# Attention and two mixture-of-experts layers: separate key and query sources, later gates, two token tiles by a product

## The chip, the cores and the metric

The kernel runs on one core of one Trainium2 chip. The time is that of one execution on the device in microseconds; the profiled execution has records of TensorE (PE, with its weight loads PEld), VectorE (DVE), ScalarE (ACT), GpSimd (POOL), and of the issues on SyncE's queue (SPq) and GpSimd's (POOLq).

## The reference

Three stages follow each other. Inputs are float32: q, k, v of 4 batches x 8 heads x 576 positions x 64, and s of 4 x 8 x 576.

```python
scores = q @ k.T / sqrt(64)
cum    = cumsum(max(s, 0))
bias   = -(cum[:, None] - cum[None, :])
scores = where(causal, -1e9, scores + min(bias, 0))
x      = softmax(scores) @ v              # as 2304 tokens x 512
h      = x @ w_in                         # 512 x 2048
x2     = (h * clip(h + 3, 0, 6) / 6) @ w_out   # 2048 x 512
logits = x2 @ w_gate                      # 8 experts
# the (token, expert) logits in falling order; a token goes to the first
# expert with room; each expert has room for 288 tokens
out[token] = max(x2[token] @ w1[e], 0) @ w2[e]  # 512 x 1024 x 512
```

## The kernel before

All products run in 16-bit parts: a float32 value is split into a high part (scaled by 64) and a low part, and three products (high x high, high x low, low x high) are summed in PSUM.

**Order.** The kernel is Python that emits instructions; a list scheduler of the tile framework then fixes the order on each engine when the program is built. Priority is the order of emission; an instruction whose inputs or buffer slots are expected later lets others go ahead. A block under `tc.high_priority` is put before what was emitted up to 20000 places earlier, `tc.issue_after(x)` (in `behind`) keeps an instruction behind `x` on its own engine. On the chip each queue then runs in its fixed order. So that stages overlap, `merge` (line 62) takes turns between generators, each of which yields the cost of what it has emitted: the one whose share of its total or budget is smallest goes next, a negative yield makes a stream rest for so many ns of the others' work, and a yielded condition blocks it until it holds.

**Attention.** A pair of heads of one batch is a unit n (16 pairs, 9 blocks of 128 rows). In step t (line 751, 18 steps), `row_stage` works on pair t, `col_stage` on t - 1, `pv_stage` on t - 2, and `prep(t + 1)` (line 234) is emitted ahead of them. `prep` builds from the loaded q and k one source tile `kq` (one buffer) with three parts of 9 x 128 columns: the low product's keys with constants, the keys with their cumulative sums CT, and the queries; a second tile `qb` (two buffers) takes the queries for the low product. One DMA transpose (line 253, 27 blocks of 128 x 128) makes `kqT` of `kq`. `row_stage` (line 286) makes the scores by rows, takes maxima on VectorE, writes them into `qb`, and a transpose of 9 blocks makes `qB` (line 334). `col_stage` (line 342) makes the scores by columns, with the maxima subtracted by the product itself, and the exponentials; `pv_stage` (line 392) the outputs, and a transpose of 10 blocks (line 442) makes `xT`, the input of the MLP. Loads of the next pairs are emitted by `between` (line 723) at the end of `row_stage`. All loads and transposes are issued on SP's queue.

**MLP and weights.** `prologue` (line 670) loads the 16 raw blocks of w_in and w_out (1 MB each) and decodes them to 16-bit parts (`decode`, line 495; the low part on GpSimd in line 517), with a budget for each step (PB, line 18). `mlp` (line 634) takes units u of 256 tokens: eight `h_step`s (line 548: 24 products of 256 columns, line 556) and two `x2_tile`s (line 591: 48 products of 512 columns, lines 598 to 600; the output goes to `xo`, two slots, from there to DRAM as `x2d` and, for the first ten tiles, through a transpose to the gate). Its budget in a step is FILL = 15500. An x2 tile waits for each half of w_out as it is decoded. What is left of the MLP after the attention runs alone.

**Gates.** For the last eight tiles the logits are taken from the MLP's hidden values by w_out x w_gate, so that routing can begin before x2 is there. `gates` (line 685) makes that product for 16 blocks of w_out: `gate_product` (line 522) issues two DMA transposes of 4 blocks (line 527) into `wT` (one slot), rests 2500 ns, and emits 8 small matmuls (lines 531, 532). GB = 1200 is its budget in a step, GT0 = 2 the first step in which it has one; a block also waits until its part of w_out is decoded.

**Experts.** `route` and `tail` (lines 952 and 1032) pick the 288 tokens of each expert, under high priority, beside the last eight x2 tiles. `gather(0)` fetches the first expert's tokens from `x2d` (three indirect DMAs on GpSimd), `tokens(0)` transposes them to `xt` (line 1119), behind the weight loads emitted before it. To start before the last tile is stored, `x2d` holds zeros for tile 17 (line 853); its tokens, always the last of the list, are put in by a product with a 0/1 matrix `lastsel` (128 x 128, lines 1052 to 1057 and 1208 to 1213), then the tile is stored for the other experts. Line 1128 is the experts' matmul, line 1106 the low part of their weights on GpSimd; `load` and `convert` (lines 1081, 1096) bring the weights through three staging slots, and the load of the second expert's third block, the last ahead of the xt transposes, waits for the fourth block of the first expert to be converted.

## Time and profile before

| | |
|---|---|
| three timed runs | 930.39, 931.59, 936.60 us; median 931.59 |
| profiled execution | 931.17 us, of which the span from first to last instruction 929.4 us |
| busy | PE 834.4 us (90%), DVE 568.3 (61%), POOL 472.6 (51%), ACT 374.9 (40%) |
| mean granted TensorE clock | 0.949 |

The profile is one execution. Busy times of an engine are the union of its instructions; matmuls are pipelined, so a busy PE need not be at its peak. In rows of a group the number behind the bar is idle time just before the instruction and what ended it. Where a row reads `[11.41 <-DMA kqT<-kq]`, the engine stood idle for 11.41 us until that DMA had landed. A granted clock of 1.00 is 2.4 GHz, 0.50 is 1.2 GHz, and a value between is a mean over a stretch.

### The profile page before, as it was taken

Reading aid. Unit: us, or ns where it says so; the run is one execution under the profiler, and the core shown is the slowest. Engines: PE = TensorE matmul, PEld = TensorE weight load, DVE = VectorE, ACT = ScalarE, POOL = GpSimd, SP = SyncE. Lnnn points to the kernel's source line nnn. Section 1 sums busy time; section 2 is a strip of 40 time slices with the busy share of each in tenths; the row PEclk is TensorE's granted clock in tenths of the full one; section 3 lists DMA queues with packets and bytes.
Section 4 is the critical chain, followed back from the end, with each engine's and each line's share of the span. In section 5 each row is a group of like instructions: output and inputs, shape, how many; then the busy total and the mean of one; then the engine's idle time right before and its main releaser. Section 6 shows DMA issues by size and latency. Waiting matters only on the chain. (4 is left out here: it accounts for less than half of the span.)

```text
span 929.4 us, 21469 instructions
## 1 busy us (share of the span) xinstructions
PE 834.4 (90%) x8553; PEld 595.1 (64%) x8553; DVE 568.3 (61%) x1705; ACT 374.9 (40%) x704; POOL 472.6 (51%) x485
## 2 busy tenths in 40 slices
PE   1688678777899999999999999999979999999996
PEld 0356457544565875866958988444447777778885
DVE  7988889875555564541356455675757877772221
ACT  2576655544344554544202222002214554455641
POOL 1466656655253564563433333003346787788951
PEclk9986778989789999999999999999989999999998
DMA  7888888789844645323220000032355765777820
GB/s 181 193 207 208 187 176 231 155 156 199 169 86 102 129 90 104 63 41 63 28 52 7 2 1 1 13 128 100 104 157 152 209 186 162 207 242 203 207 68 26
DMA packets 225524, 116.04 MB, mean 125 GB/s; under 512 B 202224, under 2 KB 202224, under 8 KB 225424
## 3 DMA queue, kind: packets, MB, share of 16 engines
q1 hardware_dynamic: 222352, 105.24, 48.1%
q0 software_dynamic: 3072, 9.44, 3.3%
q8 instruction: 67, 1.10, 0.5%
q14 instruction: 33, 0.27, 0.1%
HBM read 69.30 MB, written 9.70 MB: 85 GB/s over the span
## 5 line engine op out<-in xcount | busy, mean ns | idle before, releaser
L556 PE MATMUL mm<-xT,W 128*128 128x256 f16 (+3 forms) x2304 | 209.7, 251 | 6.1 <-DVE g L564 6.1
L1106 POOL TENSOR_TENSOR W<-stg,W 128x512 bf16<-128x512 f32 x128 | 145.0, 1159 | 100.7 <-ACT W L1104 99.8
L556 PEld LDWEIGHTS <-W 128*128 128x128 f16 (+1 forms) x2304 | 177.9, 99 | 22.9 <-DVE g L564 4.0
L1128 PEld LDWEIGHTS <-W 128*128 128x128 f16 (+1 forms) x1536 | 145.5, 98 | 42.5 <-issue 6.4
L367 POOL TENSOR_TENSOR eh<-e,eh 128x512 f16<-128x512 f32 (+1 forms) x100 | 105.5, 1070 | 99.5 <-ACT eh L365 96.6
L577 POOL TENSOR_TENSOR g<-g,g 128x512 f16<-128x512 f32 x72 | 85.5, 1187 | 125.7 <-DVE g L576 112.9
L284 PE MATMUL sc<-kqT 96*128 96x64 f16 (+10 forms) x480 | 104.7, 303 | 32.8 <-DMA kqT<-kq 18.2
L599 PE MATMUL mm<-W,g 128*128 128x512 bf16 x288 | 110.2, 383 | 3.3 <-POOL W L517 3.2
L600 PE MATMUL mm<-W,g 128*128 128x512 f16 x288 | 110.4, 384 | 0.0
L598 PE MATMUL mm<-W,g 128*128 128x512 f16 x288 | 109.6, 383 | 0.7 <-DVE g L564 0.7
L1128 PE MATMUL mm<-xt,W 128*128 128x288 f16 x768 | 105.1, 290 | 5.4 <-DVE xt L1213 4.6
L1128 PE MATMUL mm<-ht,W 128*128 128x288 f16 x768 | 102.6, 286 | 0.0
L562 ACT ACTIVATE r<-mm,three 128x512 f32<-128x512 f32 x72 | 49.4, 686 | 124.3 <-PE mm L556 116.5
L284 PEld LDWEIGHTS <-kqT 96*128 96x128 f16 (+5 forms) x768 | 54.5, 110 | 67.7 <-issue 27.2
L298 DVE TENSOR_REDUCE mx<-sc 128x1 f32<-128x384 f32 (+2 forms) x144 | 69.6, 511 | 38.0 <-PE sc L295 20.5
L364 ACT ACTIVATE e<-sc 128x512 f32<-128x512 f32 (+1 forms) x112 | 59.4, 538 | 70.0 <-PE sc L352 58.1
L564 DVE SCALAR_TENSOR_TENSOR g<-r,mm 128x512 f32<-128x512 f32 x72 | 49.3, 685 | 53.4 <-ACT r L562 52.8
L419 PE MATMUL pv<-v,eh 128*128 128x65 f16 (+1 forms) x480 | 71.4, 209 | 6.0 <-DVE x L432 6.0
L1104 ACT ACTIVATE W<-stg 128x512 f16<-128x512 f32 x128 | 75.4, 621 | 0.0
L421 PE MATMUL pv<-v,eh 128*128 128x65 f16 (+1 forms) x480 | 70.6, 205 | 1.8 <-POOL eh L367 1.8
L420 PE MATMUL pv<-v,eh 128*128 128x64 f16 (+1 forms) x480 | 71.0, 207 | 0.0
L365 ACT ACTIVATE eh<-e 128x512 f16<-128x512 f32 (+1 forms) x112 | 60.9, 570 | 13.9 <-PE pv L421 11.6
(225 smaller groups left out, 1370.3 us busy)
## 6 DMA issues: line engine op xcount, KB each, us to landing
stg<-in_moe_w_dram SPq DMA_DIRECT2D x32, 1024.0 KB
raw<-in_moe_w_in_dram SPq DMA_DIRECT2D x8, 1024.0 KB
raw<-in_moe_w_out_dram SPq DMA_DIRECT2D x8, 1024.0 KB
x2d<-xo SPq DMA_DIRECT2D x18, 256.0 KB
ldq<-in_q_dram SPq DMA_DIRECT2D x32, 128.0 KB
ldk<-in_k_dram SPq DMA_DIRECT2D x32, 128.0 KB
ldv<-in_v_dram SPq DMA_DIRECT2D x32, 128.0 KB
ldq<-in_q_dram SPq DMA_DIRECT2D x16, 32.0 KB
```

What stands on the lines that cost most here:

```text
L284: nc.tensor.matmul(o, x[0:kq], y[0:kq], start=start, stop=stop)
L367: eng.tensor_tensor(t[:, 1], e, t[:, 0], op=OP.subtract)
L419: nc.tensor.matmul(oj[:, 0:65], e[0], vv[:, 0:65], start=a, stop=False)
L420: nc.tensor.matmul(oj[:, 0:64], e[0], vv[:, 66:130], start=False, stop=False)
L556: nc.tensor.matmul(p[:, f, at:at + w], wsl(wt, ft)[:, c * 128:(c + 1) * 128], XT[b][:, c, hl, i:i + w], start=(n == 0), stop=(n == 3 * KC ...
L577: nc.gpsimd.tensor_tensor(g[:, 1].rearrange("p f x -> p (f x)"), g32, g[:, 0].rearrange("p f x -> p (f x)"), op=OP.subtract)
L598: nc.tensor.matmul(p, g[:, 0], wsl(woh, f), start=(f == 0), stop=False)
L599: nc.tensor.matmul(p, g[:, 0], wsl(wol, f), start=False, stop=False)
L600: nc.tensor.matmul(p, g[:, 1], wsl(woh, f), start=False, stop=(f == FT1 - 1))
L1104: nc.scalar.activation(h, x, AF.Copy)
L1106: nc.gpsimd.tensor_tensor(l, x, h, op=OP.subtract)
L1128: nc.tensor.matmul(p, wt[:, c, o * 128:(o + 1) * 128], x(hl, c), start=(n == 0), stop=(n == last))
```

## The change

The source tile `kq` becomes `kk` (keys only, two parts, one buffer), and `qb` becomes `qq` (two parts: the queries and those for the low product, two buffers). `kk` is transposed by a DMA of 18 blocks before the queries are worked on, the first part of `qq` by one of 9 blocks after; the maxima go into its second part, which is transposed as before. The other half of the head dimension now stands in each part, with the same sum. The gates' budget becomes 2500 a step, from step 12 on; the pause is dropped, and `wT` uses the two slots of `xo`. Tiles 16 and 17 are both left out of the first gather, and both are put in by products, with a matrix of 256 and one of 128 columns, in PSUM slots of the output stage; the transposes of the first expert's tokens and these products come under high priority. The three output slots `yo` become one ring of three.

```diff
--- before.py
+++ after.py
@@ -32,7 +32,7 @@
 DEFER = 8
 R0 = 3
 WAFT = 1
-GB = 1200.0
+GB = 2500.0
 LG = 14
 P1, GAP = 4, 0
 FL, RPOS, VPOS, PP = 0, 1, 1, 0
@@ -41,7 +41,7 @@
 WLD, XLD, KCP, QCP, CTE = 0, 0, 0, 0, 2
 HX = 0
 HE = 2
-GT0 = 2
+GT0 = 12
 RD = 0
 AH = 3
 RN = 2
@@ -172,19 +172,18 @@
     nc.vector.tensor_copy(later8[0:64], later[0:64, 0:64])
     nc.vector.tensor_copy(later8[64:128], later[0:64, 0:64])
 
-    KQ, QB = [], []
+    KK, QQ = [], []
     for i in range(2):
-        t = att.tile([128, 9, 128], F16, name=f"qb{i}", bufs=1)
-        nc.vector.memset(t[:, :, 96:99], C15)
-        nc.gpsimd.memset(t[:, :, 101:128], 0.0)
-        QB.append(t)
+        t = att.tile([128, 2, 9, 128], F16, name=f"qq{i}", bufs=1)
+        nc.vector.memset(t[:, :, :, 96:99], C15)
+        nc.gpsimd.memset(t[:, :, :, 99:128], 0.0)
+        QQ.append(t)
     for i in range(KB):
-        t = att.tile([128, 9, 3, 128], F16, name=f"kq{i}", bufs=1)
-        nc.vector.memset(t[:, :, 2, 96:99], C15)
-        nc.vector.memset(t[:, :, 0, 99:101], C15)
-        nc.gpsimd.memset(t[:, :, 0, 101:128], 0.0)
-        nc.gpsimd.memset(t[:, :, 1:3, 99:128], 0.0)
-        KQ.append(t)
+        t = att.tile([128, 9, 2, 128], F16, name=f"kk{i}", bufs=1)
+        nc.vector.memset(t[:, :, 1, 99:101], C15)
+        nc.gpsimd.memset(t[:, :, 1, 101:128], 0.0)
+        nc.gpsimd.memset(t[:, :, 0, 99:128], 0.0)
+        KK.append(t)
     V = []
     for i in range(2):
         vt = att.tile([128, 9, 132], F16, name=f"v{i}", bufs=1)
@@ -199,7 +198,7 @@
         nc.vector.tensor_scalar(st, st, 0.0, None, op0=OP.max)
         cu = att.tile([B * H, S], F32, name="cu", tag="ldv", bufs=1)
         nc.vector.tensor_tensor_scan(cu, st, z.to_broadcast([B * H, S]), 0.0, op0=OP.add, op1=OP.max)
-        c3 = [att.tile([B * H, S], F16, name=f"c3{r}", tag=("kqT", "qB", "qB")[r], bufs=(KTB, QBB, QBB)[r]) for r in range(3)]
+        c3 = [att.tile([B * H, S], F16, name=f"c3{r}", tag=("kT", "qB", "qB")[r], bufs=(KTB, QBB, QBB)[r]) for r in range(3)]
         for r in range(3):
             nc.vector.tensor_copy(c3[r], cu)
             if r < 2:
@@ -232,26 +231,23 @@
             (nc.vector, None, nc.gpsimd)[e].tensor_copy(o, x)
 
     def prep(n):
-        qb, kq = QB[n % 2], KQ[n % KB]
-        ak, qa = kq[:, :, 0:2], kq[:, :, 2]
+        kk, qq = KK[n % KB], QQ[n % 2]
         qf, kf = LD.pop(("q", n)), LD.pop(("k", n))
-        kh, qh = ak[:, :, 1, 0:64], qa[:, :, 0:64]
+        kh, qh = kk[:, :, 0, 0:64], qq[:, 0, :, 0:64]
         nc.scalar.activation(kh, kf, AF.Copy, scale=SC)
-        if n >= LK:
-            nc.scalar.activation(kf, kf, AF.Copy, scale=SC)
-        low(ak[:, :, 0, 32:96], kf, kh, n < LK)
-        copy(CTE, ak[:, :, :, 96:99], CT[:, n].unsqueeze(2).to_broadcast([128, 9, 2, 3]))
-        copy(KCP, kq.rearrange("p s w (a x) -> p s (w a) x", x=32)[:, :, 0:7:6, :],
+        low(kk[:, :, 1, 32:96], kf, kh, True)
+        copy(CTE, kk[:, :, :, 96:99], CT[:, n].unsqueeze(2).to_broadcast([128, 9, 2, 3]))
+        copy(KCP, kk.rearrange("p s w (a x) -> p s (w a) x", x=32)[:, :, 2:5:2, :],
              kh.rearrange("p s (a x) -> p s a x", x=32))
+        t = att.tile([128, 9, 2, 128], F16, name="kT", bufs=KTB)
+        pin(nc.sync.dma_start_transpose(out=t.rearrange("p s w x -> p (s w) x"), in_=kk.rearrange("p s w x -> p (s w x)")))
         nc.scalar.activation(qh, qf, AF.Copy, scale=SC)
-        if n >= LQ:
-            nc.scalar.activation(qf, qf, AF.Copy, scale=SC)
-        low(qa[:, :, 64:96], qf[:, :, 32:64], qh[:, :, 32:64], n < LQ)
-        low(qb[:, :, 0:32], qf[:, :, 0:32], qh[:, :, 0:32], n < LQ)
-        copy(QCP, qb[:, :, 32:96], qh)
-        t = att.tile([128, 9, 3, 128], F16, name="kqT", bufs=KTB)
-        pin(nc.sync.dma_start_transpose(out=t.rearrange("p s w x -> p (s w) x"), in_=kq.rearrange("p s w x -> p (s w x)")))
-        QK[n] = [t]
+        copy(QCP, qq[:, 1, :, 32:96], qh)
+        low(qq[:, 0, :, 64:96], qf[:, :, 0:32], qh[:, :, 0:32], True)
+        low(qq[:, 1, :, 0:32], qf[:, :, 32:64], qh[:, :, 32:64], True)
+        qa = att.tile([128, 9, 128], F16, name="qaT", bufs=KTB)
+        pin(nc.sync.dma_start_transpose(out=qa, in_=qq[:, 0].rearrange("p s x -> p (s x)")))
+        QK[n] = [t, qa]
 
     def vprep(n):
         vt, vf = V[n % 2], LD.pop(("v", n))
@@ -284,7 +280,7 @@
         nc.tensor.matmul(o, x[0:kq], y[0:kq], start=start, stop=stop)
 
     def row_stage(n):
-        ka, qt = QK[n][0][:, :, 1], QK[n][0][:, :, 2]
+        ka, qt = QK[n][0][:, :, 0], QK[n][1]
         mx = att.tile([128, 11], F32, name="mx")
 
         def rows(o, h, i0, j0, j1, mask):
@@ -326,7 +322,7 @@
         nc.tensor.matmul(d_, identb, later8, start=False, stop=True)
         top(mx[:, 10:11], d_)
         top(mx[:, 8:9], mx[:, 9:11])
-        qb, nm = QB[n % 2], a[:, 64:73]
+        qb, nm = QQ[n % 2][:, 1], a[:, 64:73]
         nc.vector.tensor_scalar(nm, mx[:, 0:9], -1.0 / C15, None, op0=OP.mult)
         nc.vector.tensor_copy(qb[:, :, 99], nm)
         nc.vector.tensor_tensor(qb[:, :, 100], nm, qb[:, :, 99], op=OP.subtract)
@@ -340,8 +336,8 @@
         return t.rearrange("p a w -> p (a w)").bitcast(F32)
 
     def col_stage(n):
-        t, qb = QK.pop(n)
-        kb, ka, qa = (t[:, :, i] for i in range(3))
+        t, qa, qb = QK.pop(n)
+        ka, kb = t[:, :, 0], t[:, :, 1]
 
         def cols(o, h, j, i0, i1):
             x = (slice(None), 8, slice(h * 64, (h + 1) * 64)) if j == NB else (slice(None), 4 * h + j)
@@ -521,11 +517,10 @@
 
     def gate_product(fs):
         for f in fs:
-            o = wts.tile([128, 2, KC, 128], F16, name="wT", bufs=1)
+            o = wts.tile([128, 2, KC, 128], F16, name="wT", tag="xo", bufs=2)
             o = (o[:, 0], o[:, 1].bitcast(BF))
             for t, w in zip(o, (woh, wol)):
                 nc.sync.dma_start_transpose(out=t, in_=wsl(w, f))
-            yield -DL[2]
             p = psum.tile([128, 16], F32, name="tp", tag="tp", bufs=TPB)
             for c in range(KC):
                 nc.tensor.matmul(p, o[0][:, c, :], wgh[:, c, :], start=(c == 0), stop=False)
@@ -604,8 +599,8 @@
         xo = wts.tile([128, 2, DM], F16, name="xo", bufs=2)
         GT["xo", t] = nc.scalar.activation(xo[:, 0], p, AF.Copy).ins
         nc.vector.tensor_tensor(xo[:, 1], p, xo[:, 0], op=OP.subtract)
-        if t == NT - 1:
-            GT["last"] = xo
+        if t >= NT - 2:
+            GT["last", NT - 1 - t] = xo
         else:
             store_x2(t, xo)
         if t < NT - DEFER:
@@ -850,7 +845,8 @@
 
     none = late.tile([128, 2, DM], F16, name="none", tag="xg", bufs=3)
     nc.gpsimd.memset(none, 0.0)
-    store_x2(NT - 1, none)
+    for t in range(NT - 2, NT):
+        store_x2(t, none)
     khl = late.tile([128, 3, NT, E8], F32, name="khl")
     pref = near([NT, E8], "pref")
 
@@ -1050,11 +1046,15 @@
         nc.vector.tensor_tensor(e3, b3(slotn, NT, 1), b3(part, 3, 2), op=OP.is_equal)
         nc.vector.tensor_tensor(e3, e3, b3(m, 3, 2), op=OP.mult)
         if ph == 0:
-            for j, x in ((1, RW - 128 % RW), (2, 0)):
-                w = RW - x
-                o = 0 if j == 1 else 128 - RW
-                nc.vector.tensor_tensor(lastsel[:, o:o + w], ohr[:, NT - 1, x:],
-                                        e3[:, NT - 1, j:j + 1].to_broadcast([128, w]), op=OP.mult)
+            for k, sel in enumerate(lastsel):
+                o = 0
+                for j in range(3):
+                    x = max(0, CAP - 128 * (k + 1) - j * RW)
+                    w = RW - x
+                    if w > 0:
+                        nc.vector.tensor_tensor(sel[:, o:o + w], ohr[:, NT - 1 - k, x:],
+                                                e3[:, NT - 1 - k, j:j + 1].to_broadcast([128, w]), op=OP.mult)
+                        o += w
         rhs = rt([128, NT, 2, 3], "rhs", F16)
         nc.vector.tensor_tensor(rhs[:, :, 0, :], e3, b3(tokc, 3, 2), op=OP.mult)
         nc.vector.tensor_scalar(rhs[:, :, 1, :], e3, tokp, None, op0=OP.mult)
@@ -1069,7 +1069,7 @@
         IDX[ph] = idx
 
 
-    lastsel = late.tile([128, 128], F16, name="lastsel")
+    lastsel = [late.tile([128, 128 * (k + 1)], F16, name=f"lastsel{k}") for k in range(2)]
     SCAT = []
     spacer = late.tile([1, 1], F32, name="spacer")
     half = KC * FM // 2
@@ -1158,7 +1158,7 @@
                 for hl in range(2):
                     nc.tensor.matmul(p[:, d * 128:(d + 1) * 128], yt[d][:, hl, j * RW:(j + 1) * RW], ident,
                                      start=(hl == 0), stop=(hl == 1))
-            yo = (wts, wts, ffn)[j].tile([RW, DM], F32, name="yo", tag=("wT", "x2T", "yo")[j], bufs=1)
+            yo = ffn.tile([RW, DM], F32, name="yo", bufs=3)
             nc.scalar.activation(yo, p, AF.Copy, scale=1.0 / (6.0 * SC))
             nc.gpsimd.memset(spacer, 0.0)
             st_ = nc.gpsimd.indirect_dma_start(out, bass.IndirectOffsetOnAxis(ap=IDX[ph][:, j:j + 1], axis=0), yo, None)
@@ -1202,15 +1202,21 @@
         sp = load(1, i - 1, sp) if i else load(0, 3, sp)
     g_stack.close()
     ffn = ctx.enter_context(tc.tile_pool(name="ffn", bufs=1))
-    store_x2(NT - 1, GT["last"])
-    sp = tokens(0, sp)
+    with tc.high_priority(offset=HP):
+        sp = tokens(0, sp)
     xt = XTS[0]
-    for hl in range(2):
-        p = mm_tile([128, KC, 128])
-        for c in range(KC):
-            nc.tensor.matmul(p[:, c], GT["last"][:, hl, c * 128:(c + 1) * 128], lastsel, start=True, stop=True)
-        x = xt[:, KC * hl:KC * (hl + 1), CAP - 128:]
-        nc.vector.tensor_tensor(x, x, p, op=OP.add)
+    for k in (1, 0):
+        last, w = GT["last", k], 128 * (k + 1)
+        store_x2(NT - 1 - k, last)
+        with tc.high_priority(offset=HP):
+            for c0 in range(0, 2 * KC, 512 // w):
+                cs = range(c0, c0 + 512 // w)
+                p = cpsum.tile([128, len(cs), w], F32, name="pick", tag="y", bufs=YB)
+                for c in cs:
+                    nc.tensor.matmul(p[:, c - c0], last[:, c // KC, c % KC * 128:(c % KC + 1) * 128], lastsel[k],
+                                     start=True, stop=True)
+                x = xt[:, cs.start:cs.stop, CAP - w:]
+                nc.vector.tensor_tensor(x, x, p, op=OP.add)
     for ph in range(E8):
         more = ph + 1 < E8
         if more:
```

## Rows read from the trace of the kernel before

**Rows 1.** The page: TensorE's busy tenths and granted clock in 40 slices of 23.2 us.

```profile
PE   1688678777899999999999999999979999999996
...
PEclk9986778989789999999999999999989999999998
```

**Rows 2.** Windows by step: us, PE, PEld, DVE, ACT, POOL, clock, DMA, GB/s.

```profile
135.00:181.00 46.00, 38.56 (x376) 30.79 (x373) 41.49 (x70) 24.47 (x41) 30.03 (x25) 0.88 0.81 201
181.00:217.00 36.00, 27.02 (x279) 15.85 (x280) 25.61 (x51) 17.32 (x33) 22.54 (x19) 0.91 0.79 153
217.00:247.00 30.00, 24.11 (x206) 13.35 (x204) 18.68 (x39) 13.38 (x25) 9.53 (x9) 0.83 0.90 181
247.00:288.00 41.00, 37.07 (x379) 26.17 (x376) 18.82 (x43) 14.80 (x24) 17.78 (x16) 0.92 0.51 94
313.00:338.00 25.00, 25.00 (x449) 22.88 (x446) 16.64 (x38) 13.90 (x25) 16.11 (x16) 1.00 0.50 99
```

**Rows 3.** Waits of TensorE, whole span: total us, times, longest us.

```profile
PE sc L284 <- DMA kqT<-kq: 18.2, 4, 11.4
...
PE tp L531 <- DMA wT<-W: 14.1, 8, 4.1
...
PE mm L599 <- POOL W L517: 3.2, 4, 1.0
```

**Rows 4.** Transpose issues on SP by tile: duration ns min/median/max, first and last start.

```profile
L253 SPq DMA_TRANSPOSE kqT<-kq x16: 4022/4366/6678, 13.9 to 366.1; - x16
...
L334 SPq DMA_TRANSPOSE qB<-qb x16: 1271/1327/2571, 31.0 to 412.4; - x16
...
L527 SPq DMA_TRANSPOSE wT<-W x32: 1188/1212/2415, 144.9 to 255.4; - x32
```

**Rows 5.** Timeline of the start: start us, length us, engine, line, operation, idle before.

```profile
13.86 4.17 SPq L253 DMA_TRANSPOSE kqT<-kq  x1
...
19.94 0.50 PE L284 MATMUL sc<-kqT 99*128 99x384 f16 x1 [11.41 <-DMA kqT<-kq]
...
20.00 0.68 ACT L246 ACTIVATE kq<-ldq 128x576 f16<-128x576 f32 x1 [6.79 <-DMA kqT<-kq]
...
30.61 0.50 PE L284 MATMUL sc<-kqT 99*128 99x384 f16 x1 [3.18 <-DMA kqT<-kq]
```

**Rows 6.** Timeline of SP's queue in step 12.

```profile
312.77 1.29 SPq L334 DMA_TRANSPOSE qB<-qb  x1
...
322.12 0.96 SPq L144 DMA_DIRECT2D ldq<-in_q_dram  x2
...
327.08 0.62 SPq L145 DMA_DIRECT2D ldk<-in_k_dram  x1
...
338.16 1.28 SPq L334 DMA_TRANSPOSE qB<-qb  x1
```

**Rows 7.** Timeline at the longest wait for wT.

```profile
197.83 2.51 SPq L527 DMA_TRANSPOSE wT<-W  x2
...
204.21 0.19 PE L531 MATMUL tp<-wgh,wT 128*128 128x16 f16 x1 [4.12 <-DMA wT<-W]
```

**Rows 8.** Timeline from the last x2 tile to the first expert.

```profile
675.73 0.37 SPq L1092 DMA_DIRECT2D stg<-in_moe_w_dram  x1
...
682.94 4.24 SPq L1119 DMA_TRANSPOSE xt<-xg  x3
...
684.25 0.40 PE L1211 MATMUL mm<-lastsel,xo 128*128 128x128 f16 x4 [0.66 <-ACT xo L605]
...
688.90 0.69 DVE L1213 TENSOR_TENSOR xt<-xt,mm 128x512 f16<-128x512 f16 x1 [3.89 <-DMA xt<-xg]
...
689.64 0.40 PE L1128 MATMUL mm<-xt,W 128*128 128x288 f16 x1 [4.27 <-DVE xt L1213]
```

**Rows 9.** Windows of 4 us after it, columns as in rows 2.

```profile
688.00:692.00 4.00, 2.02 (x8) 1.23 (x9) 3.04 (x13) 0.00 (x0) 1.28 (x2) 0.55 0.25 78
692.00:696.00 4.00, 4.00 (x21) 2.69 (x20) 2.19 (x5) 1.69 (x4) 3.20 (x4) 0.59 0.71 175
```


## The prediction, made before the changed kernel ran

> **What bounds the kernel now.** I read the page's slices first. From the fourteenth slice on TensorE is at 9 tenths or more but for one dip (a 7, late) and the last slice, and its clock digit is 9 (which is 90% or more); the holes and the low clock stand in the first thirteen slices, up to 302 us [rows 1]. So the second half is a queue of TensorE work with nothing to hide it behind: whatever idle time or low clock goes away anywhere ends the kernel earlier by as much, and whatever idle time is added costs as much. The question is only where TensorE stands still, and on what.
>
> The windows cut by attention step answer where. From 135 to 181 us VectorE is busy 41.5 of 46 us: that stretch is VectorE's, and TensorE's 7.4 idle us there are its shadow. From 181 to 288 (steps 8 to 10) VectorE is busy only 59%, and TensorE still stands idle 9.0 + 5.9 + 3.9 = 18.8 us, at granted clocks of 0.91, 0.83 and 0.92. From 313 to 338 it is busy 25.0 of 25.0 us at clock 1.00, with the DMA engines at half load [rows 2].
>
> The waits say on what: 14.1 us, eight times, at line 531 (gate products waiting for wT); 18.2 us, four times, for kqT; 3.2 us for the decoded output weights of line 517 [rows 3]. wT's 32 transposes are issued between 144.9 and 255.4 us [rows 4], which is just the stretch with spare VectorE time, so these waits are not in another engine's shadow.
>
> **The change part by part.** The sum is made against the profiled execution: span 929.4 us, 931.17 us in all, and the median of the three timed runs is 931.59, so the two can be read as one.
>
> *Gates later.* They may start at step 12 instead of 2 (before, in fact, when their weights are decoded: the first wT is issued at 144.9 us, in step 7 [rows 4]). The matmuls themselves cost the same wherever they stand. What goes is at most the 14.1 us of waits, and with them the low clock: what it took from the busy time of steps 8 to 10 is 0.09 x 27.0 + 0.17 x 24.1 + 0.08 x 37.1 = 9.5 us [rows 2]. Upper end 23.6. Not all of it: x2 products also wait for the decode (line 517, 3.2 us already [rows 3]), which runs on VectorE, ScalarE, GpSimd and the raw loads, and becomes the next thing late once TensorE comes earlier. It gains a little itself, since the wT issues no longer stand between the raw loads on SP's queue. Lower end 4. I take 14, a little over half.
>
> *What the gates cost in their new place.* Budget 2500 at 216 a product puts 12 of the 16 products into step 12, and the 2500 ns pause between transposes and product is gone. A pair of wT transposes holds SP for 2.51 us [rows 7]; step 12 would then ask of SP 12 x 2.51 = 30.1 us for wT, some 4.4 for the kT and qaT transposes, 1.3 for qB and as much for xT [rows 4], and 5.6 for the nine loads (322.12 to 327.70): 42.7 us, in a step that lasts 25.4 us from qB to qB [rows 6]. So up to 17.3 us of TensorE time are at risk. Against that, the order on each engine is fixed beforehand by expected readiness, so MLP matmuls, of which there are plenty, go ahead of a gate product whose wT is still on its way; wT has two slots instead of one; the DMA engines are at 0.50 instead of 0.79 to 0.90 [rows 2]; and no raw load is in front. In the longest wait the pair's issue ended at 200.34 and the product started at 204.21, 3.9 us later, behind a 1 MB raw load [rows 7]; after the first kqT the same step took 1.9 us (18.03 to 19.94) [rows 5]. Between 0 and 17.3 I take 4, about a quarter of the waits that 16 products have now. Sharing the slots with xo adds nothing I can see while u = 2 only runs its h steps; if an x2 tile falls into it, its eviction waits for a product, which the second mm bank covers.
>
> *Keys and queries apart.* The counts of ScalarE, VectorE and GpSimd instructions per pair stay: two activations, three low parts, two copies, one CT copy. The 27 blocks of kqT become 18 and 9. A kqT issue takes 4.0 to 4.4 us, a 9-block one 1.27 to 1.33 [rows 4], three of which are 4.0: the split itself is free on SP. What it gives: keys leave before the queries are worked on, so that after the last source write 1.3 us of issue remain instead of 4.2; and, with two query buffers, the next pair's queries no longer wait for the last kqT, as ScalarE does until 20.00 us [rows 5]. At the start: kqT issue 13.86 to 18.03, first row product at 19.94 after 11.41 us of waiting [rows 5]. The key source needs the cumulative sums, so it is ready no earlier; 18 blocks take 2.7 us instead of 4.17: 1.4 us. The second pair waits 3.18 us at 30.61 [rows 5], of which I take half, and half of the remaining 18.2 - 11.4 - 3.2 = 3.6 [rows 3]: 1.4 + 1.6 + 1.8, about 5 us. Bounds: 9 if the whole step comes earlier, and a loss of 2 if VectorE, the busiest engine up to 181 us, only meets the same work in a worse order.
>
> The Trainium skill has a rule against this part. "DMA: Bandwidth & Descriptors", section "Rules for kernel authors", wants many small transfers put together into one large one, and its section "Anatomy of one DMA" gives each DMA (on GpSimd's path) a fixed 2.0 us. By it the 16 additional transposes would ask for 32 us more; the rows above show no fixed part on SP, so the sum goes by them, and the rule is left as a rival.
>
> *The last two token tiles by a product.* Now: gather, xt transposes issued 682.94 to 687.18, landed by 688.90, add 0.69 us, first expert product at 689.64 after 4.27 us of idle time [rows 8]; then 8 us at clocks 0.55 and 0.59, with 6.0 us of busy time, so 2.6 lost [rows 9]. After: the gather waits for the store one tile earlier. But the xt transposes stay queued behind the load of the second expert's third block, issued at 675.73 when its staging slot comes free [rows 8], and that is not moved. So: issue 676.1 to 680.3, landed by 682.0, four adds of the 256-wide part (2.8 us) to 684.8, the last tile's low part (0.7), two adds (1.4), so the first product at about 687 instead of 689.6. Gain 2.6, perhaps half of the clock loss, less up to 1 us for eight products of double width (eight of 128 columns are two groups of 0.40 us now [rows 8]): I take 3. Bounds: 7 if idle time and low clock vanish; a loss of 3 if the gather stays behind the GpSimd subtractions and the four new adds (2.8 us) simply come on top.
>
> *At nothing:* the three yo slots in one ring instead of three tags (as many as before); one more store of zeros, on an idle queue; the memsets at the start, before GpSimd has work; three more selection products on VectorE beside x2 matmuls, under 1 us.
>
> Sum: -14 + 4 - 5 - 3 = -18, so 931.2 - 18 = 913.
>
> **The rivals.** *Slower: SP cannot feed the gates.* If in truth only one slot is free at a time, each product has issue and landing on TensorE's path: 2.51 + 1.9 = 4.4 us every 25.4 / 12 = 2.1 us, a wait of 2.3 us for each of the 16, 37 us; the clock then falls as it did in steps 8 to 10, by about a tenth over 70 us, 7 more. Against the 22 us gained elsewhere: 22 us slower, 953. It decides once these waits and their clock pass 22 us. For it: the two-step crowding above and the pause left out. Against it: TensorE waited only at 8 of 16 products even with one slot and full DMA queues [rows 3].
>
> *Another limit fills the early gap.* In steps 8 to 10 the decode and its loads set the pace (DMA 0.79 and 0.90), so that region gives 4, the start 2, the end of the x2 tiles 1, and the new place costs 3: 4 us faster, 927. For it: the line 517 waits. Against: VectorE at 59%.
>
> *The split has a price* (the skill's rule): an additional landing of 1.9 us at each of the four direct waits for kqT, 7.6 us, turns the start from -5 into +2.6: 921. Only the nine-block issues speak, and against it.
>
> *All of it comes:* 23.6 + 9 + 7 and no new waits: 892.
>
> **How the numbers follow.** Forecast 0.55, with a range of its own of 903 to 922; slower by SP 0.12; another limit 0.18; price of the split 0.05; all of it 0.10. The range 897 to 930 leaves out the SP rival and about half of the last case, some 0.17. About 1% (9.3 us, below 922.3) is what a measurement of this kernel can tell from no change. Faster by more: 0.95 of the forecast (0.52), the last case (0.10), a quarter of "another limit" (0.045): 0.67. Slower: 0.12. Within: 0.21.
>
> **What would show it.** Right: no wait for wT before 290 us, steps 8 to 10 together under 95 us instead of 107, and clocks there near 1; SP showing 12 wT pairs in one step, with waits at the gate products under 8 us in all; first row product near 18.5 us; xt issued near 676 and the first expert product near 687. Wrong: line 517, 564 or raw loads taking over in steps 8 to 10; waits of over 17 us for wT in steps 12 and 13, or a clock below 1 there; attention transposes standing behind wT on SP; xt still issued after 682.

## The result and the profile after

The kernel after takes 946.85 us (median of 4 runs, 943.76 to 951.52), the kernel before beside it 933.38 (4 runs, 930.39 to 936.6): ratio 1.0124, interval 1.0094 to 1.0155. That is 1.2%, some 11.6 us, slower; the forecast was 18 us faster. The profiled execution took 945.55 us, span 943.8 us, granted clock 0.939.

First the windows of after, cut at its own steps, to be held against [rows 2]. Columns: window, its length, busy time of PE, PEld, DVE, ACT and POOL with the number of instructions, granted clock, DMA share, GB/s.

```profile
185.00:210.00 25.00, 19.50 (x170) 10.70 (x170) 22.66 (x37) 13.34 (x26) 16.31 (x14) 0.95 0.67 147
210.00:243.00 33.00, 25.82 (x201) 13.84 (x202) 22.32 (x42) 14.78 (x26) 15.40 (x13) 0.84 0.67 150
243.00:278.00 35.00, 34.79 (x387) 25.80 (x389) 18.96 (x40) 15.46 (x28) 18.52 (x17) 1.00 0.40 83
305.00:340.00 35.00, 29.49 (x491) 26.34 (x489) 15.79 (x43) 13.06 (x24) 15.94 (x15) 0.90 0.69 123
340.00:380.00 40.00, 29.96 (x292) 16.59 (x296) 12.83 (x37) 11.19 (x21) 11.14 (x11) 0.87 0.66 115
```

Steps 8 to 10 now end at 278 us instead of 288, and the hole has moved: from 305 to 380 us, steps 12 and 13, TensorE stands idle 5.5 + 10.0 us and the clock is 0.90 and 0.87, where before it was busy without a break at 1.00. The two steps last 35 and 40 us instead of 25 each. TensorE's waits between 305 and 380 us (us in total, times, longest) have the names of [rows 3], in a new place:

```profile
PE tp L526 <- DMA wT<-W: 6.5, 5, 4.1
PE tp L527 <- DMA wT<-W: 5.0, 7, 1.2
PE tp L526 <- DVE gf L528: 3.4, 2, 2.3
```

SP's queue in the same steps shows what feeds them, to be held against [rows 6] (start, duration, issue):

```profile
304.96 1.30 SPq L330 DMA_TRANSPOSE qB<-qq  x1
...
316.48 2.64 SPq L523 DMA_TRANSPOSE wT<-W  x2
...
319.86 2.50 SPq L523 DMA_TRANSPOSE wT<-W  x2
...
323.76 16.05 SPq L523 DMA_TRANSPOSE wT<-W  x10
339.86 1.32 SPq L330 DMA_TRANSPOSE qB<-qq  x1
```

From one qB up to the next there are 14 rows, the ones left out included; added up they take 33.8 of 34.9 us, 21.2 of them in rows of wT (14 transposes), and the next qB stands right behind ten of them. A row of several joins short gaps, and the long one holds a wait of SP for a product of TensorE, as SP's own waits in that stretch show:

```profile
SPq L523 <- PE sc L322: 2.4, 1, 2.4
```

So a step in which SP issues almost without a break cannot be shorter than what is asked of SP, and where SP does stand still, it waits for TensorE, which waits for SP elsewhere.

How much this place costs is read best between two outputs of x2 tiles, the fourth and the fifth; the work between them is otherwise the same. The timeline of ScalarE in after:

```profile
294.66 0.58 ACT L600 ACTIVATE xo<-mm 128x512 f16<-128x512 f32 x1
371.47 0.60 ACT L600 ACTIVATE xo<-mm 128x512 f16<-128x512 f32 x1 [3.44 <-DMA ldv<-in_v_dram]
```

The same rows in a run of this kernel without any gates (below):

```profile
294.69 0.58 ACT L592 ACTIVATE xo<-mm 128x512 f16<-128x512 f32 x1
345.25 0.58 ACT L592 ACTIVATE xo<-mm 128x512 f16<-128x512 f32 x1
```

76.8 against 50.6 us: 26.2 us in one stretch. Of these, 15.2 are idle time (15.5 less 0.3 in the run without gates), 6.8 clock (0.10 x 29.49 + 0.13 x 29.96), and 3.4 the sixteen products themselves, at 0.21 us each (eight matmuls about 0.026 us apart). From the fifth tile to the tenth both take 127.5 us: nothing is won back and nothing more is lost.

At the end of the x2 tiles the change does what it should; to be held against [rows 8, 9]:

```profile
690.65 0.37 SPq L1092 DMA_DIRECT2D stg<-in_moe_w_dram  x1
691.08 5.39 SPq L1119 DMA_TRANSPOSE xt<-xg  x3
...
702.51 0.40 PE L1128 MATMUL mm<-xt,W 128*128 128x288 f16 x2 [0.19 <-DVE xt L1219]
```

The xt transposes leave right behind the staged load, as was said; the last x2 output is at 700.5, the first expert product 2.0 us later instead of 6.0 (683.6 to 689.6 before), and the clock stays at 1.00.

### The profile page after: what moved, and what is told of

It is laid out like the page before. It is cut to its first block, busy times and chain, and to the rows that moved or that the text cites. A ratio compares the mean times of both kernels' runs of the same rounds, so it can differ in the third digit from the quotient of the medians.

```text
span 943.8 us, 21453 instructions
## 1 busy us (share of the span) xinstructions
PE 831.6 (88%) x8521; PEld 595.6 (63%) x8561; DVE 574.6 (61%) x1711; ACT 374.5 (40%) x704; POOL 475.9 (50%) x485
## 5 line engine op out<-in xcount | busy, mean ns | idle before, releaser
L551 PE MATMUL mm<-xT,W 128*128 128x256 f16 (+3 forms) x2304 | 205.1, 248 | 7.5 <-DVE g L559 7.4
L551 PEld LDWEIGHTS <-W 128*128 128x128 f16 (+1 forms) x2304 | 177.4, 99 | 23.6 <-issue 9.0
L363 POOL TENSOR_TENSOR eh<-e,eh 128x512 f16<-128x512 f32 (+1 forms) x100 | 108.0, 1093 | 110.3 <-ACT eh L361 96.3
L593 PE MATMUL mm<-W,g 128*128 128x512 f16 x288 | 111.1, 387 | 11.6 <-ACT W L512 5.8
L595 PE MATMUL mm<-W,g 128*128 128x512 f16 x288 | 112.1, 390 | 2.1 <-issue 0.4
L1128 PE MATMUL mm<-xt,W 128*128 128x288 f16 x768 | 103.2, 286 | 3.5 <-DVE ht L1142 2.4
L594 PE MATMUL mm<-W,g 128*128 128x512 bf16 x248 | 95.9, 388 | 5.4 <-POOL W L513 5.3
L280 PE MATMUL sc<-kT,qaT 99*128 99x384 f16 (+2 forms) x192 | 51.0, 350 | 24.1 <-DMA kT<-kk 11.2
L280 PE MATMUL sc<-qaT,kT 96*128 96x64 f16 (+5 forms) x288 | 57.3, 267 | 9.3 <-DVE mx L294 7.9
```

The source lines that it names most:

```text
L280: nc.tensor.matmul(o, x[0:kq], y[0:kq], start=start, stop=stop)
L363: eng.tensor_tensor(t[:, 1], e, t[:, 0], op=OP.subtract)
L551: nc.tensor.matmul(p[:, f, at:at + w], wsl(wt, ft)[:, c * 128:(c + 1) * 128], XT[b][:, c, hl, i:i + w], start=(n == 0), stop=(n == 3 * KC ...
L593: nc.tensor.matmul(p, g[:, 0], wsl(woh, f), start=(f == 0), stop=False)
L594: nc.tensor.matmul(p, g[:, 0], wsl(wol, f), start=False, stop=False)
L595: nc.tensor.matmul(p, g[:, 1], wsl(woh, f), start=False, stop=(f == FT1 - 1))
```

## The experiments

Ratios are to the kernel before, run beside it on the same chip.

**Moving the gates back.** After, with the three lines of the gates' place as they were; everything else of the change stays, the shared slots too.

```diff
-GB = 2500.0
+GB = 1200.0
-GT0 = 12
+GT0 = 2
+            yield -DL[2]
```

> The changed kernel with the gates as before (from step 2, budget 1200, the 2500 ns pause back; wT stays in the slots of xo). Theory A, the gates' new place costs more than their old one: between the fourth and fifth x2 tile the changed kernel loses 26.6 us, and up to the fourth tile it had gained 11.8 of its 10.3 by the gates' absence, so this one comes to 946.9 - 26.6 + 11.8 = 932 us. Rival B, the split of keys and queries or the last two tiles is at fault: 944 or more.

922.34 us, ratio 0.9923 (0.9894 to 0.9952), faster still than theory A's 932. The rest of the change gains; the gates' place loses 2%. Without the pause the time is the same:

> The kernel after with the gates' old place (budget 1200 from step 2), but without the pause of 2500 ns. Theory (the pause only shifts the product among other work): within 3 us of the run with the pause, 920 to 926 us. Rival (the pause is what hid the transposes): 930 or more, with more waits for wT than the 12.5 us there.

922.67 us, 0.9922 (0.9893 to 0.9951).

**The place alone.** The kernel before with the gates part and the shared slots (and the `yo` ring), and then with the two constants only:

```diff
-GB = 1200.0
+GB = 2500.0
-GT0 = 2
+GT0 = 12
```

> The kernel before with the gates' part alone (step 12, budget 2500, no pause, slots of xo, the yo ring). Theory A: 933.4 + 26.6 - 11.8 = 948 us. Rival B: 933 or less, as the 14.1 us of early waits go.

> The kernel before with two numbers changed and nothing else: the gates' budget 2500 instead of 1200 and their first step 12 instead of 2. The wT tile keeps its one slot of its own, and the pause of 2500 ns between transposes and product stays. Theory A (the new place costs, wherever wT lies): slower than before by 8 us or more, so 938 us or more, with waits for wT at the gate products between 300 and 390 us. Rival (the place is fine, and the loss is that wT takes the slots of the x2 tiles' outputs and that the pause is gone): within 1% of before or faster, 915 to 935 us, and no wait for wT above 8 us in all.

941.36 us, 1.0120 (1.0094 to 1.0145), and 946.80 us, 1.0194 (1.0166 to 1.0223). Two constants slow the kernel by 18 us. With one slot of its own and the pause, the place costs more than with two slots and none, so neither the sharing nor the missing pause is the cause. What these two constants win first is seen at the fourth x2 tile, in the kernel before and then in the one with the two constants:

```profile
304.98 0.58 ACT L605 ACTIVATE xo<-mm 128x512 f16<-128x512 f32 x1
289.71 0.58 ACT L605 ACTIVATE xo<-mm 128x512 f16<-128x512 f32 x1
```

Up to there the gates' leaving wins 15.3 us (12.7 in the run with the whole gates part, where that tile leaves at 292.3); behind it more than that is lost.

**No transposes in the new place, or none that is waited for.** First the products all read the wT of the first block (30 of 32 transposes left out); then all 32 are issued, but the products read `wsl(w, f)` itself:

```diff
-                nc.tensor.matmul(p, o[0][:, c, :], wgh[:, c, :],
+                nc.tensor.matmul(p, wsl(woh, f)[:, c * 128:(c + 1) * 128], wgh[:, c, :],
```

> The changed kernel with the gate transposes of the first block alone, used by all 16 products (30 of 32 transposes are left out, so the gate logits are not those of the reference; the products stay where they are). If the transposes are what the new place lacks (SP's queue or their landing), the waits and the low clock go, 22 us: 925. Rival C, the products themselves (their PSUM bank, the reduce behind each, their place on TensorE) cost it: 943 or more.

> The kernel after, with all 32 wT transposes issued as there, but the gate products read the 128 columns of the untransposed rows instead of wT, so no product waits for a transpose (the gate logits of the last eight tiles are not the reference's). Theory A1 (the loss is the gate products standing on TensorE until their transpose has landed, and the low clock behind it): as fast as with one transpose, 919 to 927 us. Rival A2 (the loss is the transposes' traffic on SP's queue, which delays what attention has there): 938 to 947 us, as after. Between the two, each has its share in proportion.

921.93 us, 0.9920 (0.9890 to 0.9949), and 945.92 us, 1.0181 (1.0151 to 1.0211). This pair was the surprise of the study: without the transposes the loss is gone, yet without a single wait for them it is all there. The timeline of the second kernel, SP's rows and then two of VectorE's:

```profile
299.30 14.03 SPq L523 DMA_TRANSPOSE wT<-W  x10
313.38 1.35 SPq L330 DMA_TRANSPOSE qB<-qq  x1
314.82 5.16 SPq L523 DMA_TRANSPOSE wT<-W  x4
320.03 1.32 SPq L249 DMA_TRANSPOSE qaT<-qq  x1
321.44 3.53 SPq L243 DMA_TRANSPOSE kT<-kk  x1
...
316.70 0.33 DVE L231 COPY qq<-qq 128x576 f16<-128x576 f16 x1 [11.26 <-DMA qB<-qq]
...
327.77 0.76 DVE L223 SCALAR_TENSOR_TENSOR kk<-ldk,kk 128x576 f16<-128x576 f32 x1 [9.33 <-ACT kk L237]
```

And TensorE's waits in the same stretch:

```profile
PE tp L526 <- DVE gf L528: 14.9, 2, 8.0
PE sc L280 <- DMA qB<-qq: 6.6, 1, 6.6
```

The maxima for this qB were written at 302.7 us (its last write, line 328, ends there), and it left at 313.4, behind ten wT transposes that nobody waited for. TensorE then waits for qB itself (6.6 us), and for gate sums that stand on VectorE behind copies which wait for qB and kT (14.9 us). The traffic on SP is enough; whether TensorE sees it as a wait for wT or for something else is a matter of the order.

**Other places and another queue.** Three products a step instead of twelve (GB = 600 instead of 2500); from step 16, behind all of the attention's own transposes but the last two xT (GT0 = 16 instead of 12); and the wT transposes issued by ScalarE (`nc.scalar.dma_start_transpose`), in the place of after.

> The changed kernel with budget 600 in place of 2500: three products a step over steps 12 to 17 in place of twelve in one. If it is the crowding (12 x 2.5 us of wT issues in a 25 us step), three pairs (7.5 us) fit beside the 12 us of other issues and most of 22 us goes: 925 to 930. Rival D, each product waits because the pause is gone, wherever it stands: 940 or more.

> The kernel after with the gates' first step 16 instead of 12: all but two of the 32 wT transposes then stand in SP's order behind the last pair's qB, and no kT, qaT or load of a pair is left for them to delay. Theory (the loss is the in-order queue of SP: 32 issues of about 1.4 us, 45 us, ahead of transposes that the attention waits for): most of the loss goes, 917 to 930 us. Rival (any place after the decode costs the same, since TensorE is then always busy): 938 us or more.

> The kernel after with the wT transposes issued on ScalarE's queue instead of SP's, nothing else. Theory (what costs is that they stand in SP's queue, ahead of qB, qaT and kT): the waits for qB and kT go; if an issue holds ScalarE as long as SP, ScalarE gets 45 us more work over steps 12 and 13, where it has 24 us in 75, and the kernel comes to 922 to 938 us. Rival (it is the DMA engines that are overloaded by transposes, whoever issues them): 941 to 948, as after.

928.93 us, 0.9996 (0.9972 to 1.002); 942.73 us, 1.0141 (1.0117 to 1.0166); 955.92 us, 1.0282 (1.0257 to 1.0306). Spreading halves the price: 1.4% over the run without gates (0.9856, below) instead of 2.7%. The second refutes my narrower theory, that the wT transposes only hurt as far as they delay the attention's. From step 16 on there is little left for them to delay, and TensorE waits for wT itself, as its waits in that run show:

```profile
PE tp L527 <- DMA wT<-W: 8.9, 10, 2.6
PE tp L526 <- DMA wT<-W: 5.9, 7, 2.1
```

And its windows there:

```profile
405.00:425.00 20.00, 15.86 (x143) 8.12 (x145) 2.14 (x8) 4.17 (x7) 5.36 (x6) 0.91 0.63 116
425.00:445.00 20.00, 16.49 (x237) 12.60 (x236) 4.08 (x13) 6.65 (x12) 6.28 (x6) 0.91 0.59 96
445.00:465.00 20.00, 12.93 (x192) 11.43 (x192) 4.06 (x14) 1.37 (x2) 2.31 (x2) 0.74 0.51 88
```

14.7 us idle and 6.3 us of clock (0.09 x 15.86 + 0.09 x 16.49 + 0.26 x 12.93): the same price in another coin. The third is the worst of all, above what either theory gave, and SP's own waits name the reason:

```profile
SPq L330 <- DMA wT<-W: 29.6, 4, 15.0
SPq L249 <- DMA wT<-W: 5.6, 2, 4.4
SPq L438 <- DMA wT<-W: 5.3, 1, 5.3
```

SP's transposes (qB, qaT, xT) wait until ScalarE's have landed, so the second queue adds no room. And it holds ScalarE besides; here behind four issues that took 9.7 us:

```profile
369.86 0.68 ACT L237 ACTIVATE kk<-ldk 128x576 f16<-128x576 f32 x1 [14.60 <-issue]
```

The Trainium skill, "DMA: Bandwidth & Descriptors", section "DMA Transpose (X-bar)", has the rule behind this: of two streams that transpose, the later must wait for the earlier one's completion, since in flight together they can corrupt each other. The trace agrees as far as it goes: 40.5 us of such waits, and no pair in flight together was tried.

**Gate products without DMA transposes.** The blocks are transposed by TensorE, eight products with the identity for each gate product, evicted by ScalarE; in the old place and in the new.

```diff
+            for t, w, one in zip(o, (woh, wol), (ident, identb)):
+                p = psum.tile([128, KC, 128], F32, name="tw", tag="tp", bufs=TPB)
+                for c in range(KC):
+                    nc.tensor.matmul(p[:, c], wsl(w, f)[:, c * 128:(c + 1) * 128], one, start=True, stop=True)
+                nc.scalar.activation(t, p, AF.Copy)
```

> The kernel after with the gates in their old place, and the blocks of w_out transposed by TensorE (products with the identity, 8 of 128 columns for each gate product, evicted by ScalarE in two pieces) instead of by DMA: no wT transpose is left on SP's queue. Theory (the transposes on SP's queue are what the gates cost, and TensorE's 128 small products, about 0.06 us each, 8 us, fall into idle time): 912 to 920 us, faster than the run with the gates in the old place. Rival (the one slot for the pieces makes TensorE wait for ScalarE 32 times): 925 us or more.

> The same product by TensorE, in the new place (from step 12, budget 2500). Theory (the new place's loss is SP's 45 us of issues, and nothing else is wrong with it): the loss of 23 us goes, 8 us of TensorE time come on top where TensorE is always busy: 926 to 934 us. Rival (the products themselves, wherever their inputs come from, collide there): 940 or more.

927.59 us, 0.9930 (0.9902 to 0.9958), and 944.17 us, 1.0105 (1.0068 to 1.0141). In the old place it is no better than the DMA; in the new place nearly as bad, with nothing of the gates on SP. Windows of the latter:

```profile
305.00:340.00 35.00, 29.82 (x484) 26.20 (x482) 15.30 (x38) 17.89 (x33) 13.92 (x14) 0.90 0.30 61
340.00:380.00 40.00, 35.90 (x408) 22.62 (x412) 14.22 (x42) 23.80 (x44) 12.62 (x13) 0.96 0.37 71
```

9.3 us idle (7.2 of all its waits are for ScalarE's copies into wT), 4.4 of clock, and 10.3 of TensorE's own time (128 products of 128 columns, 0.054 us apart, and 128 gate products, 0.026 apart), of the 27.9 by which the stretch between the fourth and fifth tile, 293.3 to 371.7 us, exceeds that without gates. The same extra work, 1.0105 against 0.9930, costs 16 us more in the new place.

**What the old place costs.** One transposed block for all products in the old place; no gates at all (line 522's generator emits nothing, zeros stand in for its sums); and two products to one PSUM tile and one reduction.

> The kernel after with the gates in their old place and with the pause, but only the first block's two transposes, whose wT all 16 products read (30 of 32 transposes left out; the gate logits of the last eight tiles are not the reference's). It prices what the transposes take in the old place. Theory (there TensorE stood idle anyway, but the 12.5 us of waits for wT in the run with the gates in the old place are real): 8 to 12 us faster than that run, 910 to 915 us. Rival (something else, decode or VectorE, sets the pace of steps 8 to 10, and the waits are its shadow): within 3 us of that run, 919 to 925 us.

> The kernel after without the gates' work at all: no wT transposes, no gate products, zeros in their place (the logits of the last eight tiles are zero, so the routing is not the reference's). Beside the run with the gates in their old place (0.992 of before) it gives what the gates cost there, whatever place they have. Theory (in the old place the gates hold back the third and fourth x2 tile by about 9 us, which the change does win): 0.980 to 0.985 of before, 7 to 11 us below that run. Rival (they are hidden there, and the 9 us would be lost again later anyway): 0.988 to 0.995.

> The kernel after with the gates in their old place and with the pause, two products into one PSUM tile with one reduction on VectorE for both: 8 instead of 16 turns of the one PSUM slot, four transposes issued in a row. Theory (in the old place the waits lie in the shadow of the decode): no change beside the run without pairs, 0.989 to 0.995 of before. Rival (the turns of the one slot, TensorE to VectorE and back, are what costs there): 0.988 or less.

925.34 us, 0.9896 (0.9867 to 0.9925); 915.75 us, 0.9856 (0.9831 to 0.9880); 922.44 us, 0.9934 (0.9915 to 0.9954). Before took 934.31 us on the first one's chip and 929.93 on the other two's, so the ratios are the ones to compare. The fourth x2 tile's output on ScalarE, in the run with the gates moved back:

```profile
303.16 0.58 ACT L601 ACTIVATE xo<-mm 128x512 f16<-128x512 f32 x1
```

And in the run with one transposed block:

```profile
303.24 0.58 ACT L604 ACTIVATE xo<-mm 128x512 f16<-128x512 f32 x1
```

With two slots the transposes cost nothing there by the trace, whatever waits are put down to them, and nothing beyond the intervals by the ratios; the theory's 8 to 12 us were not to be had. Without them TensorE waits for the products' sums on VectorE instead, in that run up to the fourth tile:

```profile
PE tp L530 <- DVE gf L532: 7.2, 3, 3.1
```

The gates as a whole cost 0.67% there, 6 us: 0.9923 against 0.9856. With one transposed block 4 us of them are left (0.9896), so the products are not free in the old place either: the fourth tile, which leaves at 294.7 us without gates, is no earlier than 303.2. What makes up the 6 us is open; neither the transposes nor the turns of the PSUM slot account for them by the ratios.

**The other parts.** The last two tiles alone; the split alone (memory forces wT into the two slots of `xo`); those two slots alone; and the slots with the last tiles, without the split.

```diff
-            o = wts.tile([128, 2, KC, 128], F16, name="wT", bufs=1)
+            o = wts.tile([128, 2, KC, 128], F16, name="wT", tag="xo", bufs=2)
```

> The kernel before with the last two token tiles by products and the first expert's transposes under high priority, and nothing else of the change. My theory from the traces (4.3 instead of 9.7 us from the last x2 tile's output to the first expert's first activation): 4 to 7 us faster than before, about 925.5 us beside 930.5. Rival (those 5 us came of the other parts): within 2 us of before.

> The kernel before with keys and queries in separate source tiles, wT in the two slots of the x2 tiles' outputs and the output tiles in one ring (memory forces both), gates and last tiles as before. My theory: the split gives nothing up to the seventh pair (136.1 instead of 134.6 us at its maxima's transpose) and 1 to 4 us in all, so 927 to 930 us beside 930.5. Rival 1 (the split is worth the 5 us of the prediction): 924 to 926. Rival 2 (16 more transposes have a fixed price): 932 or more.

> The kernel before with wT in the two slots of the x2 tiles' outputs (and the output tiles in one ring), and nothing else: no split, gates and last tiles as before. It separates what was together in the run of the split, 0.9963 of before. Theory (that run's gain came of the second wT slot, since its waits for wT fell from 15.4 to 7.5 us while its waits for the keys' and queries' transposes stayed at 19.4 against 18.2): 0.994 to 0.998 of before. Rival (it came of the split): 0.999 to 1.002.

> The kernel before with two parts of the change alone: wT in the two slots of the x2 tiles' outputs, and the last two token tiles by products. Keys and queries stay in one source, the gates stay in their old place with the pause. Theory (the second slot gives 0.5 to 0.8%, the last tiles 0.4%, and the split nothing): 0.985 to 0.990 of before, the fastest kernel of the study that computes the reference. Rival (the split is worth something once these two are there): no better than the run with all but the gates' move, 0.991 to 0.995.

924.00 us, 0.9956 (0.9935 to 0.9977); 926.09 us, 0.9963 (0.9944 to 0.9981); 926.79 us, 0.9921 (0.9892 to 0.9949); 921.92 us, 0.9860 (0.9832 to 0.9887). The last tiles gain 4 us, where the prediction had 3. What the split seemed to gain is the second wT slot's, which alone gains more: the fourth x2 tile leaves at 299.2 us with the slots and at 299.7 with slots and split, against 305.0 before. At the start the split shifts waits rather than removes them, here before 140 us in the run of the split:

```profile
PE sc L280 <- DMA kT<-kk: 11.2, 1, 11.2
PE sc L280 <- DMA qaT<-qq: 8.2, 3, 5.4
```

19.4 us, where kqT alone had 18.2 [rows 3]. By the ratios the split costs 0.4 to 0.6%, and it gives nothing; the traces of the runs with and without it reach the first expert's first activation at the same time (684.7 us both), so I leave its price at between nothing and 6 us. Part of it can be read at the start of step 8, the eighth pair's qB, before and after:

```profile
181.63 1.73 SPq L334 DMA_TRANSPOSE qB<-qb  x1
185.21 1.31 SPq L330 DMA_TRANSPOSE qB<-qq  x1
```

In the six traces with one source that step begins between 180.3 and 182.7 us, in all those with two between 183.2 and 187.3. The last run, two small parts of the change, is by its ratio the fastest that computes the reference.

## Why the prediction was wrong

In the prediction's own terms, measured against the forecast (us; differences of ratios are taken at some 931 us):

| term | forecast | measured | from |
|---|---|---|---|
| gates leave the old place | -14 (4 to 23.6) | -9 to -15 | 1 - (0.9856 + 0.0044), no gates, less the last tiles; with the split as nothing or as 6 |
| gates in the new place | +4 (0 to 17.3) | +25 | 1.0124 - 0.9856 |
| split | -5 (-9 to +2) | 0 to +6 | above |
| last two tiles | -3 (-7 to +3) | -4 | 0.9956 |

The first two rows count the sixteen products too, which the prediction let cancel. As far as the runs can tell, they do: with 30 of the 32 transposes left out the gates cost 4 us in the old place and 6 in the new (0.9896 and 0.9920 against 0.9856).

**The step that failed is the price of the new place.** The term was +4 and measured +25. The working there was right in what is asked of SP: 12 pairs and the rest, 42.7 us in a step of 25.4. The step then did last 34.9 us, 33.8 of them in SP's rows, and seven pairs got through. What failed is the reason given for taking 4: that TensorE's order lets MLP products go ahead of a gate product whose wT is late. The order is fixed when the program is built; a product that stands there is waited for, whatever comes behind it. Nor would it have been enough: where no product waits for wT at all (1.0181), the attention's qB stands behind ten wT transposes, and TensorE waits for that. The prediction has this among the signs of being wrong, but no term of its sum for it; its other sign, over 17 us of waits for wT, did not come (11.5). The waits of the old place, "8 of 16 products even with one slot and full DMA queues", were no evidence on the new one: they lay in a stretch where TensorE had other reasons to stand still. The upper bound was wrong too: it held the excess of one step and left out the clock (6.8 us) and the second step (40 us instead of 25). What the two places do not share is the price of the transposes: nothing beyond the intervals in the old one, 19 us in the new (1.0124 against 0.9920).

**The rival "SP cannot feed the gates" came nearest**, at 953 with a chance of 0.12; measured 947. Its clock loss of 7 us was 6.8; its 37 us of waits were 15.5 us idle: it let each of 16 products wait 2.3 us, and there were twelve waits for wT, 11.5 us in all. That its total came near is in part luck: it had 44 us of price against 22 of gain, where 25 and 13 were measured. It decides, as it said, once waits and clock pass the gain. But its name covers half of it. Taking the waits away, the attention's transposes out of the way, SP out of the way, or the DMA transposes away each left a loss of some 10 us or more against before. Spread thin they lost nothing against before, but 7 us against the old place (0.9996, 0.9923); only where the transposes went without a substitute was the new place as good as the old. I read this as a lack of slack on TensorE, with SP's queue as the way in which this kernel pays for it. No run isolates that: each one that kept the transposes but took them off SP put the work on ScalarE or TensorE instead, and 7.2 of the 9.3 us idle with TensorE's transposes are for the copies out of their one PSUM slot.

**The early gain** came as forecast. Steps 8 to 10 take 93 us in after (185.2 to 277.8), under 95 as listed, against 106 before (181.6 to 288.0), and no wT is waited for there. The fourth x2 tile leaves only 10.3 us earlier (305.0 to 294.7), no later than without any gates, since step 8 begins 3.6 us later; with the two constants alone, without the split, it is 15.3. The gain adds up: idle time 18.8 to 12.9 us, clock 9.5 to 5.1 (0.05 x 19.50 + 0.16 x 25.82), and the products' own 3.4, which the forecast did not count there. The clocks are not near 1 but 0.95, 0.84 and 1.00, since the waits for the decode, named as the lower bound, took over (line 593 for the weights of line 512, 5.8 us). And about half of it was to be had in place: a second slot takes the waits at line 531 from 14.1 to 6.6 us and the fourth tile to 299.2, and what the transposes cost with two slots is nothing beyond the intervals.

**The split** was wrong in sign or worth nothing. The first kT issue was 2.72 us, as worked out (2.7), but began at 14.25 instead of 13.86, and 3.0 us instead of 1.9 passed from its end to the first row product, at 19.96 us, not 18.5; the next long wait there is for VectorE (5.7 us). That the rows show no fixed part on SP was misread: in [rows 4] four blocks take 1.21 us and nine 1.33. The sum does not hang on it, as its terms are issues measured at their own size. The fixed 2.0 us of "Anatomy of one DMA" in the Trainium skill's "DMA: Bandwidth & Descriptors", there for GpSimd's path, would by estimate have made 32 us of it; no run shows anything near that.

**The last tiles** were right in sign, size and mechanism (the xt transposes right behind the staged load), a little low, since the clock does not fall at all.

## What to carry to other kernels

Work whose waits cost nothing in a stretch where the bounding engine idles anyway pays for them in one where it does not: count there its own time, every wait and the clock behind the waits, and do not carry over waits measured in another engine's shadow. Add up what a step asks of an in-order queue; if it is more than the step lasts, the step gets longer, and an order fixed beforehand does not save it. Try the cheap half of an idea alone: here a second buffer, two lines, gave 0.8%.

## What the runs showed of the hardware

SP is held 1.26 us (median in after) by each transpose of four blocks and 2.90 by one of 18, so 32 of the small ones are some 40 us of a queue although their bytes are few (45.6 us in after, with the gaps and waits inside the rows). DMA transposes of two queues were not run beside each other: SP stood 29.6 us at qB alone until ScalarE's had landed. And idle time of TensorE costs more than its length: in the windows shown from 305 us on, or from 405 where the gates begin in step 16, with 3.5 to 10 us of it in each, the granted clock was 0.74 to 0.96, a mean of its two levels (1.2 and 2.4 GHz), and added 0.43 to 0.47 of the idle time to the price (6.8 to 15.5 us, 6.3 to 14.7, 4.4 to 9.3).
